# The last three slots of a fused attention and adapter kernel, put into one written order

## The chip, the cores and the metric

The kernel runs on one core of a Trainium2 chip. The metric is the device time of one execution in microseconds (us). Engines are named as the profile names them: PE (TensorE, matrix products; PEld is its weight load), DVE (VectorE), ACT (ScalarE), POOL (GpSimd) and SP (the queue engine that issues most DMAs). Each engine works through its own instructions in the order in which the program gives them and waits where an input is not there yet.

## What is computed

The reference is a spatial-reduction attention, followed by a mixture of eight low-rank adapters of which each token takes two. Cut to what matters:

```python
# attention: 4 batches of 12288 queries, 768 keys each, 128 channels
kv_flat = mean over 4x4 patches of kv, @ w_sr          # keys and values are the same
a = softmax(q @ kv_flat.T / sqrt(128))
x = a @ kv_flat                                        # (49152, 128)
# adapters
logits = x @ w_gate                                    # 8 experts, the best 2 of each token
w = softmax of the two chosen logits
out = x + sum over the 2 chosen e of w[e] * ((x @ A[e]) @ B[e])     # rank 16
```

## The kernel before

**The work is cut into 96 chunks of 512 tokens**, 24 to a batch. A chunk goes through these steps, and the names are those of the rows in the profile (all products are recorded on line 70, the helper `mm`):

- scores, in three units (`scores`, L293): two PE products of 512 columns into a PSUM tile `sg`, and one exponential on ACT (L309) from it into `em`. There are two `sg` tiles.
- attention (`attend`, L311): 24 PE products of 136 columns into `acc`, of which there is one. The columns are 128 channels, seven logits and the sum of the exponentials.
- normalise (`normalize`, L328): on DVE a reciprocal (L330) and a multiply over the whole chunk (L338) into `xn`, which holds x and the logits.
- the best two logits (`top`, L353, four DVE instructions MAX8), the routing (`route`, L362, four small POOL instructions L370 to L376 that make an argument and a mask), a tanh on ACT (L383) and two POOL instructions (L385, L386) that make the gate weights `gw`.
- x transposed: four PE products (`tx` below) into PSUM, a copy to SBUF.
- down (`down`, L431): four PE products with A, into PSUM.
- gate (`gate`, L436): DVE multiplies by the gate weights (L439), which gives `hg`.
- `hg` transposed, either by PE and a copy or by a DMA transpose issued from SP (`turn_dma`, `turn_alone`).
- up (`up`, L469): four PE products with B, into PSUM `d_ps`.
- finish (`finish`, L480): DVE adds x to the result (L486), and SP stores two chunks together (L491).

The small PSUM tiles of transposes, down and up come from a pool `mb` with two buffers. A tile that is to be written waits until a buffer has been read out.

**The order.** Chunks run as a pipeline over slots. In slot k the scores of chunk k are made, chunk k-1 is attended, chunk k-2 is normalised and its logits are routed, and the adapters of older chunks run in between. A loop (L651 to L790) emits the slots up to 95. The tail behind it (L792 to L934) takes what is left by hand. It attends chunk 95 and ends the adapters of chunks 92 to 95 in that order: routing of 95 on DVE (L907 to L912), the other gates on POOL, copies of transposes on ACT (`fetch_x` L837, `fetch_h` L843). Chunk 92's result is copied by ACT (`carry`, L866) and its x added by POOL (`add_there`, L870). DVE adds those of 93, 94 and 95 (`add_here`, L861). The four chunks are stored one by one (`store`, L476). Chunk 94's store is on ACT's queue and the other three are on SP's.

Slots 93, 94 and 95 begin at 346.3 us of the profiled execution, and the last compute instruction ends at 365.92 us.

Of the kernel before, what the change touches and what calls it, by code (L numbers as in the profile page):

```python
# [10 lines left out]
FP32 = mybir.dt.float32  # L11
BF16 = mybir.dt.bfloat16
# [8 lines left out]
def kernel(  # L21
# [87 lines left out]
    def load_q(g, m):  # L109
# [8 lines left out]
        keep(nc.sync.dma_start(q_f[g, m], src[:, m * S:(m + 1) * S]))  # L118

# [208 lines left out]
    def normalize(k):  # L328
# [3 lines left out]
        if m == 0:  # L332
            half = k0 % 2 if k0 >= TURN else 0
            if half == 0:
                used.append(k0)
            xg[k0] = ring[(len(used) - 1) % len(ring)][:, half:half + size[k0]]
# [23 lines left out]
    later = []  # L360

    def route(k0):  # L362
# [16 lines left out]
        later.append(lambda: gates(k0, n, eng, arg, mask))  # L379

# [99 lines left out]
    def finish(k):  # L480
# [5 lines left out]
        keep(nc.vector.tensor_tensor(osb[:, int(k == kb)], dp[k], xn[k][:, :, 0:C], op=ALU.add))  # L486
# [114 lines left out]
    done.append(NCHUNK - 5)  # L601
# [49 lines left out]
    for k in range(k1, NCHUNK):  # L651
# [100 lines left out]
        for x_ in kx[:1]:  # L752
# [5 lines left out]
            elif x_ in by_strip:  # L758
                gate(x_, strip(k, 0)[:, 1])
                turn_dma(k, *todo, (hgT, x_))  # L760
                todo = []
                up_at(k + 3, x_)
            elif k == NCHUNK - 1:
                turn_alone(x_)
                up(x_ - 1)
                finish(x_ - 1)
            else:
                gate(x_)
# [23 lines left out]
    K = NCHUNK - 1  # L792
    assert not units, units
    assert kh == [K - 3] and ku == [K - 4], (kh, ku)

    def flat(o):
        return o.rearrange("p a b -> p (a b)")[:, 0:T].rearrange("p (s c) -> p s c", s=S)

    def low(o):
        return (o.bitcast(BF16).rearrange("p a b -> p (a b)")[:, 0:T]  # L800
                .rearrange("p (s c) -> p s c", s=S))

    def bank(n=None):
        if n is None:
            return mtile([P, S, P], name="tail_ps")
        if n in banks:
            return banks[n]
        if n[0] == "a":
            t = ps_a.tile([P, S, 256], FP32, tag="acc", name="acc")
            for i in range(2):  # L810
                banks[f"a{i}"] = t[:, 2 * i:2 * i + 2]
        else:
            t = ps_s.tile([P, 2, T], FP32, tag="sg", name="sg")
            for i in range(2):
                banks[f"{n[0]}{i}"] = t[:, i:i + 1]
        return banks[n]

    banks = {}

    def spread(dst, lhs, rhs, lo=0, hi=S, transpose=False):  # L820
# [4 lines left out]
    def turn_x(k):  # L825
        ps = low(bank())
        xb = xn[k].bitcast(U16)[:, :, 1::2].bitcast(BF16)
        spread(ps, lambda s: xb[:, s, 0:C], id_bf, transpose=True)
        xT[k] = ps

    def turn_h(k, o, lo=0, hi=S):
        spread(low(o), lambda s: hg[k][:, s], id_bf, lo, hi, True)
        hgT[k, lo] = low(o)

    def fetch_x(k):
        sb = run.tile([P, S, P], BF16, tag="tt1", name="tt1")
        keep(nc.scalar.copy(sb, xT[k]))  # L837
        xT[k] = sb

    def fetch_h(k, lo=0, hi=S):  # L840
        if lo == 0:
            hgT[k] = run.tile([P, S, P], BF16, tag="tt1", name="tt1")
        keep(nc.scalar.copy(hgT[k][:, lo:hi], hgT[k, lo][:, lo:hi]))  # L843

    def part(k, o, js):
        for s in range(S):
            for j in js:
                mm(o[:, s, 0:VE], em[k][:, s, j], vx[k // NB][:, j, 0:VE],
                   start=(j == 0 and s % 2 == 0), stop=(j == J - 1 and s % 2 == 1))

    def down_into(k, o):
        hp[k] = flat(o)
        spread(hp[k], lambda s: xT[k][:, s], a_bf)

    def up_into(k, o, lo=0, hi=S):
        dp[k, lo] = flat(o)
        spread(dp[k, lo], lambda s: hgT[k][:, s], b_bf, lo, hi)

    def add_here(k, queue, lo=0, hi=S):
        osb = opool.tile([P, 2, S, C], FP32, tag="osb", name="osb")[:, 0, 0:hi - lo]  # L860
        keep(nc.vector.tensor_tensor(osb, dp[k, lo][:, lo:hi], xn[k][:, lo:hi, 0:C], op=ALU.add))  # L861
        store(queue, k, osb, lo, hi)

    def carry(k):
        osb = opool.tile([P, 2, S, C], FP32, tag="osb", name="osb")[:, 0]
        keep(nc.scalar.copy(osb, dp[k, 0]))  # L866
        dp[k] = osb

    def add_there(k, queue):
        keep(nc.gpsimd.tensor_tensor(dp[k], dp[k], xn[k][:, :, 0:C], op=ALU.add))  # L870
        store(queue, k, dp[k])

    def gate_part(k, lo=0, hi=S):
        if lo == 0:
            hg[k] = run.tile([P, S, P], BF16, tag="hg", name="hg")
        keep(nc.vector.tensor_tensor(  # L876
            hg[k][:, lo:hi].rearrange("p s (e r) -> p (s e) r", e=E),
            hp[k][:, lo:hi].rearrange("p s (e r) -> p (s e) r", e=E),
            gw[k][:, lo:hi].rearrange("p s e -> p (s e)")
            .unsqueeze(2).broadcast_to([P, (hi - lo) * E, RK]), op=ALU.mult))  # L880

    turn_x(K - 2)
    tanhs()
# [81 lines left out]
```

## Time and profile before

| | us |
|---|---|
| median of 3 runs | 371.83 (371.45 to 372.01) |
| span of the profiled execution, first to last instruction | 369.48 |
| slot 93 begins (first score product of chunk 93) | 346.3 |
| last DVE instruction ends | 365.92 |

The median is 2.35 us above the profiled execution's own span. That much lies around a span, and the profile does not show it. Times in rows are microseconds from the span's start, and mean durations are in ns. A row with `<-PE acc L70` in brackets or behind a bar says how long the engine was idle before and which instruction ended that wait. In tables by stretch each engine has its busy time and, in brackets, its number of instructions. An engine's instructions overlap by some 0.08 us each, so the sum of durations is larger than the busy time.

### The profile page before, as it was taken

How to read it: one execution, taken by the hardware profiler on the slowest of the kernel's cores; microseconds unless marked ns; L12 is line 12 of the kernel's file. 1: busy time of each engine (PE TensorE's matmuls, PEld its weight loads, DVE VectorE, ACT ScalarE, POOL GpSimd, SP SyncE). 2: the span in 40 equal slices, each digit the busy share in tenths (PEclk: the TensorE clock that was granted, in tenths of full speed). 3: DMA queues.
4: the chain of work that ended last, by engine and by line, in shares of the span. 5: the costliest groups of instructions: out<-in, count | busy, mean ns of one | idle time of the engine just before them, and what ended most of it. 6: DMA issues, size and time to landing. Idle time of an engine off the chain costs nothing.

```text
span 369.5 us, 11071 instructions
## 1 busy us (share of the span) xinstructions
PE 359.4 (97%) x4272; PEld 281.2 (76%) x4272; DVE 292.7 (79%) x923; ACT 292.8 (79%) x363; POOL 229.9 (62%) x519
## 2 busy tenths in 40 slices
PE   8899999999999999999999999999999999999993
PEld 4677788877878787787787787877777767777782
DVE  1347799887888888888888898888887777779795
ACT  1548986787878878888888888878879989898873
POOL 1110368889877677677768758756666766665442
PEclk9999999999999999999999999999999999999998
DMA  7989769999789999999999999999999999999723
GB/s 252 383 297 208 254 189 279 318 252 251 199 267 235 226 320 261 190 265 319 218 261 254 260 237 236 282 279 175 191 191 229 232 224 199 204 231 232 192 94 149
DMA packets 72869, 88.08 MB, mean 238 GB/s; under 512 B 51345, under 2 KB 51601, under 8 KB 72465
## 3 DMA queue, kind: packets, MB, share of 16 engines
q1 hardware_dynamic: 65728, 62.93, 68.3%
q0 software_dynamic: 6656, 24.12, 28.7%
q8 instruction: 33, 0.54, 0.6%
q10 hardware_dynamic: 432, 0.33, 0.3%
q14 instruction: 20, 0.16, 0.1%
HBM read 50.53 MB, written 36.70 MB: 236 GB/s over the span
## 4 chain that ended last, share of the span: by engine, by line
PE 88%; DMA 7%; DVE 2%; SPq 1%; issue 1%; ACT 0%; DVEq 0%; ACTq 0%
PE acc L70 35%; PE sg L70 32%; PE tt_ps L70 6%; PE d_ps L70 6%; PE h_ps L70 5%; DMA turn<-turn 4%; DMA kvr<-in_kv_dram 2%; DMA qf<-in_q_dram 2%; PE kpT_ps L70 1%; PE v_ps L70 1%; PE kfT_ps L70 1%; DVE xn L338 1%; SPq L102 1%; PE qT_ps L70 0%; DVE hg L876 0%
## 5 line engine op out<-in xcount | busy, mean ns | idle before, releaser
L309 ACT ACTIVATE em<-sg 128x1024 f16<-128x1024 f32 x288 | 283.3, 1022 | 58.0 <-PE sg L70 55.9
L70 PE MATMUL sg<-qT,kfT 128*128 128x512 bf16 x576 | 170.4, 379 | 0.4 <-ACT em L309 0.2
L70 PE MATMUL acc<-vx,em 128*128 128x136 f16 x2280 | 167.7, 223 | 0.1
L70 PEld LDWEIGHTS <-em 128*128 128x128 f16 x2304 | 146.7, 98 | 18.9 <-DVE xn L338 3.0
L338 DVE TENSOR_TENSOR xn<-acc,rinv 128x540 f32<-128x540 f32 x95 | 68.5, 721 | 3.3
L486 DVE TENSOR_TENSOR osb<-d_ps,xn 128x512 f32<-128x512 f32 x92 | 62.9, 689 | 2.7 <-PE d_ps L70 0.9
L541 POOL TENSOR_TENSOR kvr<-kvr 128x512 f32<-128x512 f32 (+1 forms) x48 | 56.9, 1200 | 0.5
L370 POOL TENSOR_TENSOR over<-xn,srt 128x64 f32<-128x64 f32 (+1 forms) x120 | 31.0, 279 | 36.0 <-DVE srt L358 34.4
L70 PEld LDWEIGHTS <-kfT 128*128 128x128 bf16 x576 | 45.2, 98 | 2.7 <-issue 0.6
L385 POOL TENSOR_TENSOR gw<-th,over 128x64 f32<-128x64 f32 (+1 forms) x60 | 17.3, 289 | 48.0 <-ACT th L383 47.5
L330 DVE RECIPROCAL rinv<-acc 128x4 f32<-128x4 f32 x95 | 17.3, 182 | 34.2 <-PE acc L70 31.4
L407 DVE COPY tts<-tt_ps 128x1024 bf16<-128x1024 bf16 (+1 forms) x73 | 36.9, 506 | 0.0
L70 PEld LDWEIGHTS <-xn 128*128 128x128 bf16 x296 | 22.5, 98 | 16.5 <-DVE xn L338 0.2
L358 DVE MAX8 srt<-xn 128x8 f32<-128x8 f32 x380 | 34.5, 153 | 0.1
L70 PEld LDWEIGHTS <-tts 128*128 128x128 bf16 x388 | 27.0, 98 | 7.0 <-DVE tts L407 0.4
L70 PE MATMUL h_ps<-a_bf,tts 128*128 128x128 bf16 x284 | 27.5, 219 | 0.0
L70 PE MATMUL tt_ps<-id_bf,xn 128*128 128x128 bf16 x284 | 27.4, 219 | 0.0
L376 POOL TENSOR_SCALAR over<-over 128x64 f32<-128x64 f32 (+1 forms) x60 | 19.8, 330 | 5.4
L229 POOL TENSOR_TENSOR kvr<-kvr 128x512 f32<-128x512 f32 x18 | 22.4, 1271 | 0.5 <-DMA kvr<-in_kv_dram 0.4
L439 DVE TENSOR_TENSOR hs<-h_ps,gw 128x512 bf16<-128x512 f32 x28 | 19.1, 683 | 4.5 <-POOL gw L386 4.0
L439 DVE TENSOR_TENSOR hg<-h_ps,gw 128x512 bf16<-128x512 f32 x26 | 17.9, 689 | 5.9 <-POOL gw L386 5.2
L70 PEld LDWEIGHTS <-turn 128*128 128x128 bf16 x176 | 13.0, 98 | 10.2 <-DMA turn<-turn 2.2
(98 smaller groups left out, 314.6 us busy)
## 6 DMA issues: line engine op xcount, KB each, us to landing
out_dram<-osb SPq DMA_DIRECT2D x46, 512.0 KB, 5.8
kvr<-in_kv_dram POOLq DMA_DIRECT2D x24, 512.0 KB, 6.6
kvr<-in_kv_dram SPq DMA_DIRECT2D x21, 512.0 KB, 7.7
qbf<-in_q_dram POOLq DMA_DIRECT2D x20, 512.0 KB, 7.7
qf<-in_q_dram SPq DMA_DIRECT2D x8, 256.0 KB, 7.4
kvr<-in_kv_dram SPq DMA_DIRECT2D x6, 256.0 KB, 7.5
qbf<-in_q_dram POOLq DMA_DIRECT2D x4, 256.0 KB, 5.6
out_dram<-osb SPq DMA_DIRECT2D x3, 256.0 KB, 2.3
```

Of the source, the lines that this page charges most:

```text
L70: return keep(nc.tensor.matmul(*a, **k))
L229: keep(adder.tensor_tensor(u[:, lo:hi], u[:, lo:hi], v[:, lo:hi], op=ALU.add))
L309: keep(nc.scalar.activation(o, i_, AF.Exp, bias=0.0, scale=scale))
L330: keep(nc.vector.reciprocal(ri, acc[k][:, :, VC]))
L338: keep(nc.vector.tensor_tensor(x[:, :, 0:VC], acc[k][:, :, 0:VC], ri.unsqueeze(2).broadcast_to([P, S, VC]), op=ALU.mult))
L358: keep(nc.vector.max(srt[k0][:, m, s], xn[k][:, s, C:C + E]))
L370: keep(eng.tensor_tensor(d, lg, so[:, :, i].unsqueeze(2).broadcast_to([P, n, 8]), op=ALU.subtract))
L376: keep(eng.tensor_scalar(mask, mask, 0.0, None, op0=ALU.is_ge))
L407: keep(nc.vector.tensor_copy(sb[:, lo:hi], ps[:, lo:hi]))
L439: keep(nc.vector.tensor_tensor(hg[k].rearrange("p s (e r) -> p (s e) r", e=E), hp[k].rearrange("p s (e r) -> p (s e) r", e=E), gw[k0][:, m ...
L486: keep(nc.vector.tensor_tensor(osb[:, int(k == kb)], dp[k], xn[k][:, :, 0:C], op=ALU.add))
L541: keep(nc.gpsimd.tensor_tensor(u, u, v, op=ALU.add))
```

## The change

The loop now ends after slot 92. All that it did in slots 93 to 95, and the whole hand-written tail, is replaced by one list of steps, `closing`, which a new function `last` works through. Each step names an operation, a chunk, and an engine or a PSUM pool. The order in which the program gives the steps is the order of each engine. What differs in content:

- The chunks are attended in the order 92, 95, 94, 93, and their scores are made in that order (95, 94, 93).
- Chunk 94 is normalised by four ACT activations (a copy with the reciprocal as scale, one for each 128 tokens), behind the reciprocal on DVE.
- Chunk 92's x reaches its result on PE. Four fp32 products with an identity matrix (`rx`) write x into the PSUM tile first, the up products accumulate onto it, and ACT copies the sum out (`fc`).
- The transposes of `hg` of chunks 90, 91 and 92 are DMA transposes (`hd`); before, this was so for 92, while 90 and 91 went over PE in one PSUM tile together with the x of 91 and 92, with one copy on DVE for both halves. The copies of the x of 91 and 92 (`cx`) are now for one half alone.
- The gate weights of 90, 92, 93 and 94 are made on DVE in one instruction, those of 91 and 95 by POOL. The routing of 92 is on DVE, and that of 95 is on POOL.
- All stores go through SP. Chunk 89 is finished before 88.

Steps: `sc` scores, `at` attention (a quarter), `nm` normalise, `top`, `rt` routing, `th` tanh, `gw` gate weights, `tx` and `cx` transpose of x and its copy, `dn` down, `gt` gate, `hd` DMA transpose of `hg`, `hx` and `ch` its transpose by PE and the copy, `up`, `ad` add x and store, `fc` copy out and store.

```diff
-    for k in range(k1, NCHUNK):
+    for k in range(k1, NCHUNK - 3):
...
-    turn_x(K - 2)
-    tanhs()
...
-    add_here(K, nc.sync)
+    def last(op, k, *w):
...
+        elif op == "nm":
...
+            keep(nc.vector.reciprocal(ri[:, lo:hi], acc[k][:, lo:hi, VC]))
+            if e is nc.scalar:
+                for s in range(lo, hi):
+                    keep(nc.scalar.activation(x[:, s, 0:VC], acc[k][:, s, 0:VC], AF.Copy, bias=0.0,
+                                              scale=ri[:, s:s + 1]))
...
+        elif op == "hd":
+            dst = hpool.tile([P, 1, S, P], BF16, tag="t1", name="t1", bufs=3)
+            keep(nc.sync.dma_start(dst.rearrange("c h s p -> c (h s) p"),
+                                   hg[k].rearrange("p s c -> p (s c)"), transpose=True))
...
+        elif op == "rx":
+            dp[k] = held("rx", k, lo, lambda: bank(pool))
+            for s in range(lo, hi):
+                mm(dp[k][:, s], id_f, xn[k][:, s, 0:C], start=(s == lo), stop=False)
...
+        elif op == "fc" and k >= NCHUNK - 4:
+            osb = out_of(k)
+            copy(e, osb[:, lo:hi], dp[k][:, lo:hi])
+            store(nc.sync, k, osb[:, lo:hi], lo, hi)
...
+    closing = (
+        "nm 91 - DVE; tx 90 - mb; sc 95 2; cx 90 - DVE; th 90 -; up 87 - mb; sc 95 0; "
+        "at 92 0 acc; at 92 1 acc; at 92 2 acc; sc 95 1; ad 87 -; at 92 3 acc; top 91 -; "
+        "rt 91 - POOL; gw 90 - DVE; tx 91 - mb; nm 92 - DVE; sc 94 2; dn 90 - mb; sc 94 1; "
+        "gt 90 -; at 95 0 acc; hd 90; at 95 1 acc; tx 92 - mb; sc 94 0; top 92 -; "
+        "cx 91 - DVE; cx 92 - DVE; th 91 -; at 95 2 acc; at 95 3 acc; gw 91 - POOL; sc 93 0; "
+        "up 89 - mb; rt 92 - DVE; dn 91 - mb; sc 93 1; nm 95 - DVE; top 95 -; th 92 -; "
+        "at 94 0 acc; at 94 1 acc; gt 91 -; ad 89 -; gw 92 - DVE; sc 93 2; dn 92 - mb; "
+        "hd 91; at 94 2 acc; at 94 3 acc; up 88 - sg; up 90 - mb; at 93 0 sg; rt 95 - POOL; "
+        "at 93 1 sg; th 95 -; gt 92 -; nm 94 - ACT; at 93 2 sg; hd 92; at 93 3 sg; ad 88 -; "
+        "tx 94 - mb; ad 90 -; tx 95 - mb; gw 95 - POOL; top 94 -; up 91 - acc; rx 92 - sg; "
+        "rt 94 - POOL; cx 95 - ACT; nm 93 - DVE; th 94 -; dn 95 - mb; top 93 -; cx 94 - ACT; "
+        "ad 91 -; tx 93 - sg; rt 93 - POOL; gw 94 - DVE; gt 95 -; up 92 - sg; cx 93 - ACT; "
+        "dn 94 - mb; th 93 -; hx 95 - acc; dn 93 - mb; fc 92 - ACT; gt 94 -; gw 93 - DVE; "
+        "ch 95 - ACT; gt 93 -; hx 94 - sg; up 95 - mb; ch 94 - ACT; hx 93 - mb; up 94 - sg; "
+        "ch 93 - ACT; ad 95 -; up 93 - acc; ad 94 -; ad 93 -")
```

More of the change, by code (lines that the diff above doesn't have):

```diff
@@ L790, with bank, spread @@
             add_patches(*w)
[L792 to L820, printed above, removed]
+    closed = {}
+    def bank(pool, dtype=FP32):
+        if pool == "mb":
+            return mtile([P, S, P], dtype, name="end_ps")
+        t = ps_a.tile([P, S, 256], FP32, tag="acc", name="end_ps") if pool == "acc" else ps_s.tile(
+            [P, 2, T], FP32, tag="sg", name="end_ps")
+        t = t.rearrange("p a b -> p (a b)")[:, 0:T]
+        if dtype is BF16:
+            t = t.bitcast(BF16)[:, 0:T]
+        return t.rearrange("p (s c) -> p s c", s=S)
+    def spread(dst, lhs, rhs, lo, hi, transpose=False):
         kw = dict(is_transpose=True) if transpose else {}
@@ L840, in fetch_h @@
[L840 to L853, printed above, removed]
```

215 lines of the change are left out of this document (122 added, 93 removed).

## The prediction

> **What bounds the kernel now.** I read the page first, then the chain that ended last, then busy time by stretches of the end, then single rows there.
>
> ```profile
> PE 359.4 (97%) x4272; PEld 281.2 (76%) x4272; DVE 292.7 (79%) x923; ACT 292.8 (79%) x363; POOL 229.9 (62%) x519
> ```
>
> Over the whole span PE is full, but the change touches only what follows 346.3 us. Three rows of busy time by stretches cover that end (length, then busy time and instructions of PE, PEld, DVE, ACT, POOL, then clock, DMA share, GB/s).
>
> ```profile
> 346.85:363.60 16.75, 15.44 (x205) 12.35 (x203) 15.07 (x50) 12.86 (x21) 7.18 (x28) 1.00 0.36 118
> 360.20:363.60 3.40, 2.26 (x28) 1.57 (x28) 3.16 (x14) 2.50 (x7) 1.66 (x6) 1.00 0.24 99
> 363.60:365.92 2.32, 1.03 (x12) 0.68 (x12) 1.99 (x4) 0.82 (x2) 0.68 (x1) 1.00 0.33 124
> ```
>
> In the first stretch DVE is busy 15.07 of 16.75 us, hardly less than PE. In the second, behind the last attention, it is busy 3.16 of 3.40, and PE only 2.26. The chain that ended last says the same (start, length, engine, tile, line):
>
> ```profile
> 359.61 0.69 DVE hg L876
> ...
> 362.91 0.70 DVE hg L876
> ...
> 363.66 0.41 PE sg L70 x4
> ...
> 364.15 0.59 ACT tt L843
> ...
> 365.23 0.69 DVE osb L861
> ```
>
> From 359.61 to 363.60 it runs on DVE: gate of 93, normalise of 95, gate of 95. From the end of the last gate there is a fixed run: transpose on PE, copy on ACT, up on PE, add on DVE, 2.32 us to 365.92. So the end is set by the time at which DVE ends its last gate, and after it by the stores.
>
> **The change, part by part.** First, DVE's list. Prices, from the groups by form (busy us, mean ns behind the bar) and from line 407 by itself (min, median and max ns; the shortest is one half, the longest a pair):
>
> ```profile
> L338 DVE TENSOR_TENSOR xn<-acc,rinv 128x540 f32<-128x540 f32 x95 | 68.5, 721 | 3.3
> ...
> L921 DVE SCALAR_TENSOR_TENSOR gw<-th,mk 128x32 f32<-128x32 f32 x1 | 0.2, 182 | 0.0
> ```
>
> ```profile
> L407 DVE COPY tts<-tt_ps x73: 414/416/693, 33.9 to 355.2; 128x512 bf16<-128x512 bf16 x49, 128x1024 bf16<-128x1024 bf16 x24
> ```
>
> Chunk 94's multiply leaves DVE: -0.72. The two copies of pairs (x of 91 with `hg` of 90, x of 92 with `hg` of 91) become copies of one half: 2 x (0.416 - 0.693) = -0.55. Gate weights come to DVE for four chunks where it had one (95): +3 x 0.18 = +0.55. Routing on DVE changes from chunk 95 to 92 and costs the same. Chunk 92's add was not on DVE before and is not after. Net -0.72 us, of which all lies ahead of the last gate.
>
> Second, the waits. I followed the new order on all engines from 346.3 us. An instruction starts when its engine is free and its inputs are there, with 0.03 to 0.15 us for a hand-over (a gate ends at 363.60, PE starts at 363.66). PE's groups take, by the chain of waits:
>
> ```profile
> 356.38 0.43 PE sg L70 x2
> 356.82 0.22 PE d_ps L70 x4
> 357.04 1.06 PE acc L70 x18
> 358.11 0.22 PE tail_ps L70 x4
> ```
>
> A score unit is 0.43, a quarter of an attention 0.35, four small products 0.22. What DVE waited for so far were the ends of attentions. Of the four reciprocals, the first (92) and the last (95):
>
> ```profile
> 350.12 0.18 DVE L330 RECIPROCAL rinv<-acc 128x4 f32<-128x4 f32 x1 [0.51 <-PE acc L70]
> ...
> 360.23 0.18 DVE L330 RECIPROCAL rinv<-sg 128x4 f32<-128x4 f32 x1
> ```
>
> In the new order `at 92` still starts when `nm 91` has freed `acc` (347.8) and has one score unit among its quarters instead of two groups. Its reciprocal comes at 349.9. `at 95` starts behind four groups of PE at 351.05 and ends its third quarter at 352.8, so that the second reciprocal comes at 353.3. `at 94` (354.4 to 356.7, two groups in between) gives 356.7. `at 93` goes to an `sg` tile, need not wait for `acc`, and ends at 358.5: the fourth reciprocal comes at 358.55, 1.7 us before the old one. It is then DVE that is late. Behind 358.55 stand the reciprocal and multiply of 93 (0.90), four MAX8 (0.37), the add of 91 (0.69), gate weights of 94, gates of 95 and 94, gate weights and gate of 93 (0.18 + 0.69 + 0.69 + 0.18 + 0.69), 4.4 us by durations, 4.1 with the overlap of neighbours. The last gate ends at 362.7. Worked in the same way, the old order's last gate ends at 363.43, where the trace has 363.60. So the difference is -0.75 us. It agrees with the budget: -0.72 of work and waits as before (1.7 us in the old list: 16.75 less 15.07). New waits of DVE that stand in it: 0.2 for `cx 92`, 0.13 for `gw 92` (its tanh stands behind an exponential on ACT; `gt 92` and all that follows are queued behind it), 0.1 for `top 95`.
>
> Third, what lies beside.
>
> `nm 94` on ACT: four activations of 128x135.
>
> ```profile
> L309 ACT ACTIVATE em<-sg 128x1024 f16<-128x1024 f32 x3 | 3.1, 1020 | 0.5 <-PE sg L70 0.5
> L837 ACT COPY tt<-tail_ps 128x512 bf16<-128x512 bf16 x2 | 1.2, 585 | 1.2 <-PE tail_ps L70 1.2
> L383 ACT ACTIVATE th<-over 128x32 f32<-128x32 f32 x2 | 0.4, 221 | 0.0
> ```
>
> On the line between the two activations, 135 elements take 221 + 103 x 0.805 = 304 ns. The upper bound is the copy, 0.585. Both ends: four take 1.0 us or 2.1 us, with 0.09 of overlap each. At 304 they end at 357.9, when DVE reaches `top 94` at 358.1 and PE reaches `tx 94` at 358.35. I take 304, the nearer rows, at no cost. Above 0.39 each, every 0.1 costs 0.44, at 0.59 it is 0.84. The Trainium skill, page "ScalarE: Activation LUTs", section "What ACT_TABLE_LOAD costs", adds about 93 ns for each pointer operand, which the scale is here. No row before the change has one. By that an activation would be an estimated 0.40, and the compute term would be -0.71 instead of -0.75.
>
> `rx 92`: four fp32 products. The nearest rows:
>
> ```profile
> 242.80 0.50 PE v_ps L70 x4
> ```
>
> ```profile
> L70 PEld LDWEIGHTS v_ps<-wext,kpT x48: 186/190/191, 11.4 to 271.3; 128*128 128x128 f32 x48
> L70 PE MATMUL v_ps<-wext,kpT x48: 278/278/319, 11.6 to 271.4; 128*128 128x135 f32 x48
> ```
>
> Each fp32 product is two records there, and two products take 0.50. So four take 0.95 at 128 columns. Upper end: with no overlap of loads, 8 x (0.28 + 0.19) = 3.8; lower end the 0.22 of bf16. I take 0.95, a measured stretch of the same kind. PE has it at 359.0 to 360.0, and `dn 95`, `tx 93`, `up 92`, `dn 94` are queued behind. DVE works off the add of 91 and gates meanwhile, and gate 93 has its input at 361.9, as DVE reaches it at 362.0. Cover is gone above 1.05, then it costs its excess, up to 2.7. Below 0.95 nothing is gained.
>
> `hd 90`, `hd 91`: two PE transposes (0.44) become DMA transposes, an issue of 1.2 on SP each.
>
> ```profile
> t<-h SPq DMA_TRANSPOSE x17, 6.8
> ```
>
> ```profile
> t<-h SPq DMA_TRANSPOSE x1, 2.4
> ```
>
> ```profile
> DMA to landing us min/median/max: 2.4/3.4/4.4
> ```
>
> The first is the median of all 17 such transposes, the second the only one behind 340 us (issued at 357.4), the third is of the last two. The new ones are issued at 351.5, 355.3 and 356.85, and are needed at 356.7, 358.8 and 360.4: slack 5.2, 3.5 and 3.5 from issue to landing. DMA share is 0.36 here. I take up to 3.4, at no cost. On SP the store of 88 and 89 now stands behind `hd 92`, at 358.1, and nobody waits for it.
>
> The order of chunks ahead, chunk 88 behind 89, and POOL's routing (7.18 of 16.75 busy) cost nothing: POOL has over half its time free, and loses the 1.27 us add of chunk 92.
>
> Fourth, the stores.
>
> ```profile
> 364.31 1.97 SPq L476 DMA_DIRECT2D out_dram<-osb  x3
> ```
>
> ```profile
> 365.00:365.50 0.50, 0.19 (x4) 0.01 (x1) 0.29 (x2) 0.00 (x0) 0.00 (x0) 1.00 0.70 270
> 365.50:366.00 0.50, 0.00 (x0) 0.00 (x0) 0.42 (x1) 0.00 (x0) 0.00 (x0) 1.00 1.00 369
> 367.50:368.00 0.50, 0.00 (x0) 0.00 (x0) 0.00 (x0) 0.00 (x0) 0.00 (x0) 0.50 0.78 303
> ```
>
> ```profile
> DMA to landing us min/median/max: 2.1/2.1/2.1
> ```
>
> ```profile
> DMA to landing us min/median/max: 2.4/2.4/2.4
> ```
>
> The last two rows are the landings of the store at 364.31 and of the last one, issued at 365.94. Four stores of 256 KB (three on SP, one on ACT's queue) leave within 1.6 us, the DMA share is 1.00 until shortly before 368, and the last lands at 368.34. By the order worked out, chunk 92's store leaves at 362, those of 95, 94 and 93 at 363.6, 364.2 and 365.0. At 370 to 390 GB/s a store takes 0.7, so that no queue is left for the last one. I take 2.1 for it, as for the first one before. That is -0.3. Ends: 0 (2.4 again), and -0.45 (the share of 0.70 puts the first bytes at 365.15, 0.84 behind the issue at 364.31; a lone store issued at 365.94 would begin at 366.8 and end at 367.5, and the share of 0.78 has the end at about 367.9). All on SP: an issue takes 0.35, and the adds come 0.69 apart, so nothing queues there.
>
> Sum: -0.75 - 0.3 = -1.05 us, a span of 368.4 against 369.48 of the profiled execution. The 2.35 us around the span stay. On the median: 371.83 - 1.05 = 370.8.
>
> **The rivals.**
>
> A, new waits eat it: the order is tight at `cx 92`, `gw 92`, `nm 94`, `rx 92` and gate 93 (0 to 0.2 us of slack each, `rx` 0.1). For: the slack is less than the error of my working (0.17). Against: it hit the old order's last gate to 0.17 over 17 us. If activations take 0.5 (+0.48) and the hand-overs on the way another 0.3, the sum is -0.3, and the time is 371.5. With nothing saved by the stores as well: 371.8. That is no change.
>
> B, slower: the DMA transposes of 91 and 92 land late. One mechanism: `up 91` and `up 92` wait on PE, and the down products of 95, 94 and 93 are queued behind them, then the gates. Every 0.1 us of landing beyond 3.5 costs 0.1. At 4.4, the upper of the last two, it is +0.85: 371.6. At 6.8, the median of all, +3.25: 374.0. From 4.6 on it is slower than before. For it: the median. Against it: in this stretch the share of DMA is a third, and the single one there took 2.4.
>
> C, more: DVE's waits shrink too, since PE is 1.7 us ahead at the fourth attention. Half of the 0.5 us of waits above gone and -0.45 from the stores: -1.45, 370.4. At most another 0.5 goes in hand-overs: 369.9.
>
> D, it doesn't do what it says: ACT's normalise or the identity product put a load of a table or separate loads in. At 3.8 us for `rx 92` it is +2.7 and 373.5. Against it are the 0.50 us row and the one table load in the whole trace:
>
> ```profile
> L178 ACT ACT_TABLE_LOAD x1 | 1.3, 1283 | 1.6 <-PEq L949 1.6
> ```
>
> **How the numbers follow.** 0.2% is 0.74 us, about what a measurement of this kernel can tell from no change: below 371.09 is faster, above 372.57 slower. Forecast (370.3 to 371.1): 0.48. C (369.9 to 370.3): 0.12. A (371.1 to 372.2): 0.26. B 0.09 and D 0.05, of which 0.03 together land within 0.2%: they give 0.11 of slower. So faster 0.60, same 0.29, slower 0.11. The likeliest is the forecast, 370.8. The range goes from 369.9 to 372.2: it leaves out B and D beyond that and little more, and it takes in both ends of `nm 94` and of the stores, and the first 1.3 us of `rx 92`'s excess and of late transposes.
>
> **What would show it.** In the changed kernel: the fourth reciprocal near 358.6 and DVE without gaps above 0.2 from there to the last gate, near 362.7 to 362.9; the last add ending near 365.2; four activations of near 0.31 to 0.40 between 357 and 358.5; `rx 92` within 1.0; the transposes issued near 355.3 and 356.9 landing before 358.8 and 360.4; a last store that lands 2.1 after its issue. I am wrong if PE waits for a transpose, if DVE waits more than 0.5 in one place behind 356, or if the last store takes 2.4 or more again.

## The result, and the profile after

The changed kernel takes 371.1 us (median of 22 runs) beside 372.21 for the kernel before in the same session (22 runs). The ratio is 0.9963, with a 95% interval from 0.9945 to 0.9982: faster by 0.37%, where the forecast was 0.28% (1.05 of 371.83). In a second session the same kernel gave 0.9933 [0.9901, 0.9964]. Ratios are of the fast runs alone, and three profiled executions below (the changed kernel again, 93 and 95 swapped, and the kernel before without a store) are slow ones, but the granted clock is 1.00 in every closing that is compared here. The profiled execution has a span of 368.51, where 368.4 was forecast and 369.48 stood before. So size and sign came out as forecast. The terms of the sum did not, and the experiments are about them.

First the page and busy time by stretches of the changed kernel, cut at the same events as in the prediction (length, then busy time and instructions of PE, PEld, DVE, ACT, POOL, clock, DMA share, GB/s):

```profile
PE 360.2 (98%) x4272; PEld 282.2 (77%) x4272; DVE 291.8 (79%) x925; ACT 293.6 (80%) x367; POOL 226.9 (62%) x511
```

```profile
346.94:363.22 16.28, 15.66 (x202) 12.61 (x200) 14.21 (x51) 13.65 (x25) 4.95 (x20) 1.00 0.51 138
...
363.22:365.48 2.26, 1.07 (x14) 0.67 (x12) 1.98 (x3) 0.77 (x2) 0.00 (x0) 1.00 0.55 210
```

From the reciprocal of chunk 91 to the last gate it is 16.28 us instead of 16.75. DVE's work in it fell from 15.07 to 14.21, by 0.86. (The budget had -0.72. By durations it is 0.77, and the rest is that neighbours overlap more.) But DVE now stands idle for 2.07 instead of 1.68. Only about half of the saved work turned into time. The rows of the timeline show where DVE and PE waited (start, length, engine, line, tile, and in brackets the idle time before it and what ended it):

```profile
346.94 0.17 DVE L847 RECIPROCAL rinv<-acc 128x4 f32<-128x4 f32 x1
...
349.99 0.18 DVE L847 RECIPROCAL rinv<-acc 128x4 f32<-128x4 f32 x1 [0.82 <-PE acc L70]
353.42 0.18 DVE L847 RECIPROCAL rinv<-acc 128x4 f32<-128x4 f32 x1 [0.32 <-PE acc L70]
356.89 0.17 DVE L847 RECIPROCAL rinv<-acc 128x4 f32<-128x4 f32 x1
357.09 1.16 ACT L850 ACTIVATE xn<-acc,rinv 128x135 f32<-128x135 f32 x4
358.67 0.18 DVE L847 RECIPROCAL rinv<-sg 128x4 f32<-128x4 f32 x1
359.36 0.40 PE L70 MATMUL end_ps<-b_bf,t 128*128 128x128 bf16 x4 [0.28 <-DMA t<-h]
359.59 1.11 PE L70 MATMUL end_ps<-xn,id_f 128*128 128x128 f32 x8
360.54 0.39 PE L70 MATMUL end_ps<-a_bf,tts 128*128 128x128 bf16 x4
...
360.96 1.36 DVE L902 TENSOR_TENSOR hg<-end_ps,gw 128x512 bf16<-128x512 f32 x2 [0.26 <-PE end_ps L70]
362.53 0.69 DVE L902 TENSOR_TENSOR hg<-end_ps,gw 128x512 bf16<-128x512 f32 x1
363.35 2.13 DVE L935 TENSOR_TENSOR osb<-end_ps,xn 128x512 f32<-128x512 f32 x3
```

The four reciprocals come at 349.99, 353.42, 356.89 and 358.67, each within 0.2 of the forecast. Then PE stands still for 0.28 in front of `up 91`, and the bracket names the cause: the DMA transpose of chunk 91's `hg`. The down products of 95, which are behind it on PE, are late, and DVE waits 0.26 for them. The last gate ends at 363.22, outside the forecast 362.7 to 362.9. The transpose that PE waited for, and the last store (issue to landing):

```profile
DMA to landing us min/median/max: 3.9/3.9/3.9
```

```profile
DMA to landing us min/median/max: 2.0/2.0/2.0
```

The store left at 365.51 and landed in 2.0, where the last one before took 2.4. The bytes end soon after 367, as busy time by half microseconds shows:

```profile
364.50:365.00 0.50, 0.25 (x4) 0.07 (x2) 0.35 (x2) 0.00 (x0) 0.00 (x0) 1.00 0.19 74
365.00:365.50 0.50, 0.00 (x0) 0.00 (x0) 0.48 (x1) 0.00 (x0) 0.00 (x0) 1.00 0.97 365
...
366.50:367.00 0.50, 0.00 (x0) 0.00 (x0) 0.00 (x0) 0.00 (x0) 0.00 (x0) 0.50 0.97 381
367.00:367.50 0.50, 0.00 (x0) 0.00 (x0) 0.00 (x0) 0.00 (x0) 0.00 (x0) 0.50 0.13 45
```

Three stores share that stretch now, not four. From the end of the last add to the span's end it is 3.03 us (365.48 to 368.51), where it was 3.56 (365.92 to 369.48).

**How the experiments are read.** The two ratios above, for one and the same program, lie 0.3% apart, nearly as much as the whole change. So ratios can't order the variants below. Profiled executions also differ by up to 8 us in when slots 93 to 95 begin, for kernels with the same instructions ahead of them. So I count from the start of the reciprocal of chunk 91 on DVE, which opens the closing part ("the closing" from here on) in both kernels. Of the kernel before:

```profile
346.85 0.17 DVE L330 RECIPROCAL rinv<-acc 128x4 f32<-128x4 f32 x1
```

By this measure, the kernel before and the same kernel without one store (below) agree within 0.01 us up to the last add, though one closing begins 7.5 us later than the other. The table has what each closing gave, in us after that reciprocal (end of the last gate, end of the last add, end of the span), PE's wait for chunk 91's transpose, and the landing of that transpose. The last column has the start and the duration of a DMA packet that is explained under "Why the transpose is late".

| kernel | last gate | last add | span end | span end less last add | PE waits | landing of 91 | packet |
|---|---|---|---|---|---|---|---|
| before | 16.75 | 19.07 | 22.63 | 3.56 | | | |
| changed | 16.28 | 18.54 | 21.57 | 3.03 | 0.28 | 3.9 | 9.5, 1.25 |
| changed, again | 15.94 | 18.19 | 21.24 | 3.05 | 0 | 3.6 | 9.5, 0.93 |
| normalise 94 on DVE | 16.37 | 18.63 | 21.66 | 3.03 | 0 | 3.7 | 9.6, 0.94 |
| add of 92 on DVE | 16.49 | 18.75 | 21.79 | 3.04 | 0.44 | 4.1 | 9.6, 1.32 |
| store of 92 late | 16.43 | 18.69 | 22.26 | 3.57 | 0.44 | 4.1 | 9.4, 1.42 |
| up of 91 late | 16.12 | 18.38 | 21.41 | 3.03 | 0 | 3.7 | 9.5, 0.93 |
| 93 and 95 swapped | 16.46 | 18.73 | 21.77 | 3.04 | 0.47 | 4.1 | 9.6, 1.41 |
| before, no store of 92 | 16.75 | 19.07 | 22.29 | 3.22 | | | |
| long warm-up | 15.85 | 18.11 | 21.16 | 3.05 | 0 | 2.4 | 6.9, 1.20 |
| long warm-up, add of 92 on DVE | 16.45 | 18.71 | 21.75 | 3.04 | 0 | 2.4 | 6.9, 1.27 |
| long warm-up, gate weights on POOL | 16.60 | 18.86 | 21.91 | 3.05 | 0 | 2.4 | 7.0, 1.22 |
| short products in the warm-up | 15.84 | 18.11 | 21.16 | 3.05 | 0 | 2.4 | 6.9, 0.99 |
| no warm-up | 16.27 | 18.54 | 21.59 | 3.05 | 0.29 | 3.9 | 10.4, 0.97 |

PE comes to `up 91` at 12.1 in the changed kernel, and the transpose is issued at 8.4. So the landing may take 3.7 before PE waits.

### The profile page after: what moved, and what is told of

It reads as the page before. It is cut to its first block, busy times and chain, and to the rows that moved or that the text cites. A ratio compares the mean times of both kernels' runs of the same rounds, so it can differ in the third digit from the quotient of the medians.

```text
span 368.5 us, 11062 instructions
## 1 busy us (share of the span) xinstructions
PE 360.2 (98%) x4272; PEld 282.2 (77%) x4272; DVE 291.8 (79%) x925; ACT 293.6 (80%) x367; POOL 226.9 (62%) x511
## 4 chain that ended last, share of the span: by engine, by line
PE 88%; DMA 8%; DVE 1%; SPq 1%; ACT 0%; issue 0%; DVEq 0%
PE acc L70 35%; PE sg L70 32%; PE tt_ps L70 6%; PE d_ps L70 5%; PE h_ps L70 5%; DMA turn<-turn 4%; DMA kvr<-in_kv_dram 2%; DMA qf<-in_q_dram 2%; PE kpT_ps L70 1%; PE v_ps L70 1%; PE end_ps L70 1%; DMA out_dram<-osb 1%; PE kfT_ps L70 1%; SPq L102 1%; PE qT_ps L70 0%
## 5 line engine op out<-in xcount | busy, mean ns | idle before, releaser
L341 DVE TENSOR_TENSOR xn<-acc,rinv 128x540 f32<-128x540 f32 x91 | 65.6, 720 | 3.1
L493 DVE TENSOR_TENSOR osb<-d_ps,xn 128x512 f32<-128x512 f32 x87 | 59.5, 689 | 2.7 <-PE d_ps L70 0.7
L373 POOL TENSOR_TENSOR over<-xn,srt 128x64 f32<-128x64 f32 (+1 forms) x112 | 29.2, 281 | 34.5 <-DVE srt L361 32.9
L389 POOL TENSOR_TENSOR gw<-th,over 128x64 f32<-128x64 f32 (+1 forms) x55 | 16.0, 292 | 43.0 <-ACT th L387 42.7
L411 DVE COPY tts<-tt_ps 128x1024 bf16<-128x1024 bf16 (+1 forms) x70 | 35.1, 501 | 0.0
L361 DVE MAX8 srt<-xn 128x8 f32<-128x8 f32 x364 | 33.0, 153 | 0.0
L70 PE MATMUL h_ps<-a_bf,tts 128*128 128x128 bf16 x272 | 26.3, 219 | 0.0
L70 PE MATMUL tt_ps<-id_bf,xn 128*128 128x128 bf16 x272 | 26.3, 219 | 0.0
L379 POOL TENSOR_SCALAR over<-over 128x64 f32<-128x64 f32 (+1 forms) x56 | 18.7, 333 | 5.0
L443 DVE TENSOR_TENSOR hg<-h_ps,gw 128x512 bf16<-128x512 f32 x24 | 16.5, 689 | 5.8 <-POOL gw L390 5.2
```

What stands on the lines that cost most here:

```text
L70: return keep(nc.tensor.matmul(*a, **k))
L341: keep(nc.vector.tensor_tensor(x[:, :, 0:VC], acc[k][:, :, 0:VC], ri.unsqueeze(2).broadcast_to([P, S, VC]), op=ALU.mult))
L361: keep(nc.vector.max(srt[k0][:, m, s], xn[k][:, s, C:C + E]))
L373: keep(eng.tensor_tensor(d, lg, so[:, :, i].unsqueeze(2).broadcast_to([P, n, 8]), op=ALU.subtract))
L379: keep(eng.tensor_scalar(mask, mask, 0.0, None, op0=ALU.is_ge))
L411: keep(nc.vector.tensor_copy(sb[:, lo:hi], ps[:, lo:hi]))
```

## The experiments

**Theory 1** is that of the prediction: DVE's list of work sets the last gate, so each 0.1 put on DVE costs about 0.1. **Theory 2**, the rival, is that the order of PE's groups set it (an earlier fourth attention), and that what moved off DVE was worth nothing. Beside them stand two questions: whether the stores gave what the last part of the gain needs, and why chunk 91's transpose was late.

**The changed kernel again**, unaltered.

> The changed kernel once more, unaltered, as the measure for its neighbours: span 368.5 (profiled so far), last gate at 363.2, last add ending at 365.5, last store landing 2.0 after its issue. If the DMA transpose of chunk 91 lands in 3.0 instead of 3.9 us (351.6, 355.4 and 357.0 are the issues), PE does not wait for it at 359.4, and the last gate comes 0.3 earlier: then span 368.2.

Ratio 0.9933 [0.9901, 0.9964]. This time no row has PE waiting for a transpose, and the last gate and the adds are 0.34 earlier:

```profile
351.90 0.17 DVE L847 RECIPROCAL rinv<-acc 128x4 f32<-128x4 f32 x1
```

```profile
367.15 0.69 DVE L902 TENSOR_TENSOR hg<-end_ps,gw 128x512 bf16<-128x512 f32 x1
367.97 2.12 DVE L935 TENSOR_TENSOR osb<-end_ps,xn 128x512 f32<-128x512 f32 x3
```

The last gate ends at 367.84, which is 15.94 after 351.90. The landing was 3.6 here and 3.9 in the first profile. The expectation had 3.0 for a landing without a wait, and 3.6 turned out to be early enough. One program, two closings 0.34 apart: the wait comes and goes with the landing, and where it is absent the compute term is -0.81 (16.75 to 15.94), a little more than the -0.75 of the forecast.

**Normalise 94 on DVE.**

```diff
-  ... th 95 -; gt 92 -; nm 94 - ACT; at 93 2 sg; hd 92; ...
+  ... th 95 -; gt 92 -; nm 94 - DVE; at 93 2 sg; hd 92; ...
```

> Chunk 94 is normalised on DVE again, one multiply of 0.72, instead of four activations on ACT; nothing else changes. Theory 1 (DVE's list sets the last gate): the last gate comes 0.4 to 0.6 later than in the changed kernel (0.72 of work, less some of DVE's waits), the span is 368.9 to 369.1. Theory 2 (the gain is the order of PE's work, DVE has room): the gate stays within 0.1, the span within 0.1 of 368.5.

Ratio 0.998 [0.9947, 1.0014]; the interval is too wide to tell. The closing tells:

```profile
347.79 0.17 DVE L847 RECIPROCAL rinv<-acc 128x4 f32<-128x4 f32 x1
```

```profile
363.47 0.69 DVE L902 TENSOR_TENSOR hg<-end_ps,gw 128x512 bf16<-128x512 f32 x1
```

The last gate ends at 364.16, 16.37 after. Beside the closings that also had no wait (15.94, 15.85, 15.84) that is 0.43 to 0.53 more, of 0.72 put on DVE. Theory 1 holds, with part of the work taken up by closer overlap on DVE (its busy time grew by 0.48 over the second run of the changed kernel, 14.13 to 14.61). Theory 2 has no place for it. No run has DVE's old list in the new order of PE, so what the order alone is worth is not measured.

**The add of 92 on DVE**, without the identity product and ACT's copy.

```diff
-  ... up 91 - acc; rx 92 - sg; rt 94 - POOL; ... dn 93 - mb; fc 92 - ACT; gt 94 -; ...
+  ... up 91 - acc; rt 94 - POOL; ... dn 93 - mb; ad 92 -; gt 94 -; ...
```

> Chunk 92's x is added by DVE (0.69) in the place of ACT's copy; the four identity products (0.95 on PE) are gone. Theory 1: last gate 0.4 to 0.6 later, span 368.9 to 369.1, although PE has 0.95 less to do. Theory 2 (PE sets the end): PE gets to the down products of 94 and 93 earlier, so the last gate comes up to 0.3 earlier, span 368.2.

Ratio 0.9942 [0.9912, 0.9971]. The last gate is at 16.49. PE waited 0.44 for the transpose:

```profile
359.14 0.40 PE L70 MATMUL end_ps<-b_bf,t 128*128 128x128 bf16 x4 [0.44 <-DMA t<-h]
```

Two other kernels with a wait of 0.44 and 0.47, which left `rx 92` in place, ended at 16.43 and 16.46. So beside its like this one cost 0.03 to 0.06, and alone it looked like a point for theory 2. But it changed two things: 0.69 on DVE, and 0.95 off PE right behind the wait. A PE that is late through the wait gets that time back. The pair had to be tried without the wait, which is done below.

**93 and 95 swapped** in every step of the list.

> Chunks 93 and 95 change names in the whole list: 93 is attended second and 95 last, all else is alike (same engines, same places). Theory 1 (only what each engine does, and when, counts): span within 0.1 of 368.5, same gates. If the chunk attended first matters as such (its scores, its place in memory or in a pair): another time, either way.

Ratio 0.9973 [0.9949, 0.9996], the last gate at 16.46 with a wait of 0.47. The store-late kernel, whose compute part is that of the changed kernel in its written order, ended at 16.43 with a wait of 0.44. Which chunk is attended last is worth nothing. The place in the order is what counts.

**The store of 92 late**, behind the add of 94.

```diff
-  ... dn 93 - mb; fc 92 - ACT; gt 94 -; ... ad 95 -; up 93 - acc; ad 94 -; ad 93 -
+  ... dn 93 - mb; gt 94 -; ... ad 95 -; up 93 - acc; ad 94 -; fc 92 - ACT; ad 93 -
```

> ACT's copy of chunk 92's result, and so its store, moves from before the copies of the last three transposes to behind them: four stores of 256 KB leave within 2 us again instead of three. Theory 1 with the stores' term: last gate and last add unchanged within 0.1, the last store lands 2.4 to 2.5 after its issue instead of 2.0, span +0.4 (368.9). If the term is not real: landing stays 2.0, span within 0.1.

Ratio 0.9991 [0.9954, 1.0028]. From the last add to the span's end it is 3.57, against 3.03 in the changed kernel and 3.56 before. The share of the DMA engines, by half microseconds, and the landing of the last store:

```profile
366.50:367.00 0.50, 0.04 (x1) 0.00 (x0) 0.42 (x1) 0.07 (x1) 0.00 (x0) 1.00 0.85 332
...
368.50:369.00 0.50, 0.00 (x0) 0.00 (x0) 0.00 (x0) 0.00 (x0) 0.00 (x0) 0.50 0.97 381
369.00:369.50 0.50, 0.00 (x0) 0.00 (x0) 0.00 (x0) 0.00 (x0) 0.00 (x0) 0.50 0.70 279
```

```profile
DMA to landing us min/median/max: 2.5/2.5/2.5
```

The bytes of four stores now run until after 369.3, over 2 us past the last add (367.26). One chunk's store moved behind the add of 94, and the whole second term of the sum went back. So the number of stores in the last stretch counts. In the eleven other closings of the new order, with three stores there, this part is 3.03 to 3.05.

**Before, without the store of 92** (its output is not written).

```diff
-        store(queue, k, dp[k])
```

> The kernel before, without the store of chunk 92 (that part of the output is not written); its copy and add stay. Three stores instead of four stand in the last 1.6 us. If the queue of stores costs what the changed kernel saved there: last add still at 365.9, the last store lands 1.9 to 2.1 after its issue instead of 2.4, span 369.0 to 369.2 against 369.48. If not: landing 2.4, span 369.4 to 369.5.

Ratio 1.0017 [0.9978, 1.0057]. Up to the last add nothing changed (19.07 in both). From there it is 3.22 instead of 3.56: -0.34. The last store lands in 2.0, as expected, so one store fewer gives all of the landing's 0.4, and about two thirds of the changed kernel's 0.53. The other 0.19 lies behind the last landing: the span ends 1.17 after it here and 1.11 in the kernel before, where all closings of the new order have 0.99 or 1.00. No run shows the cause of that. Chunk 94's store is on ACT's queue in the two kernels of the old order alone, which no run changes by itself.

**Up of 91 late**: behind `rx 92` and the down products of 95, and the add of 91 behind `gt 95`.

```diff
-  ... top 94 -; up 91 - acc; rx 92 - sg; ... th 94 -; dn 95 - mb; ... cx 94 - ACT; ad 91 -; ... gt 95 -; ...
+  ... top 94 -; rx 92 - sg; ... th 94 -; dn 95 - mb; up 91 - acc; ... cx 94 - ACT; ... gt 95 -; ad 91 -; ...
```

> The up products of chunk 91, which waited on PE for a DMA transpose (landing 3.9 against 3.5 of slack), go behind the identity products and the down products of 95; the add of 91 goes behind the gate of 95. If that wait was what kept the last gate at 363.2: PE has no wait for the transpose, the gate comes 0.1 to 0.3 earlier, span 368.2 to 368.4. If DVE's list sets it in any case: gate and span within 0.1.

Ratio 0.998 [0.9947, 1.0012]. No wait, with a landing of 3.7, and the last gate at 16.12. That is 0.16 before the changed kernel with its 0.28 of wait, and 0.18 behind it without. So this order costs 0.18 where there is no wait. Whether it takes a wait away this run can't show: at a landing of 3.7 the kernel with 94 normalised on DVE, which has `up 91` in its old place, does not wait either. The interval can't show a difference of this size.

**Why the transpose is late.** I looked for what lies beside it. On the page's part on DMA queues (packets, MB, share of 16 engines' span) one queue of the changed kernel has few and large packets, 16 KB each:

```profile
q8 instruction: 33, 0.54, 0.6%
```

The same table for the 5.5 us from 8.0 after the reciprocal of 91, in the changed kernel, with DMA's busy tenths and GB/s above it (40 slices of 0.14 us):

```profile
DMA  0000000000066999990000000000699982009999
GB/s 0 0 0 0 0 0 0 0 0 0 0 138 145 199 207 199 110 11 0 0 7 7 11 9 9 11 8 9 121 177 223 212 172 40 0 0 417 417 417 387
...
q8 instruction: 1, 0.02, 1.4%
```

Chunk 91's bytes come at 200 GB/s and break off. Then 6 to 11 GB/s trickle for over 1 us, then those of 92 come at 200 again. One packet of the instruction queue takes 1.4% of 16 engines for 5.5 us, that is about 1.2 us of one engine. It starts at 356.5, as the bytes of 91 begin. 0.54 MB over PE's 8544 instructions (4272 products and as many weight loads) is 63 bytes each, so one packet would be the fetch of about 260 of PE's instructions. If so, another number of PE instructions ahead moves it. At the 402 instructions in 16.28 us of this stretch, 64 more make it come 2.6 us earlier.

**Long warm-up.** The 8 products that warm PE up at the start become 40 of 102 columns each, which makes 64 more instructions.

```diff
-        for _ in range(n):
-            mm(mtile([P, T], name="spin_ps"), zero[:, 0:P], zero, start=True, stop=True)
+        m = 5 if n == 8 else 1
+        for _ in range(m * n):
+            mm(mtile([P, T], name="spin_ps")[:, 0:T // m], zero[:, 0:P], zero[:, 0:T // m], ...)
```

> The changed kernel with PE's first eight spin products of 512 columns written as forty of 102: as many columns, 64 PE instructions more at the very start, nothing else. In the runs so far the DMA transpose of chunk 91 landed 3.6 to 4.1 us after its issue, that of 90 in 2.4; with 91's a 16 KB packet of the instruction queue was under way, and the later the landing, the longer that packet. Theory 3 (that packet, a fetch of PE's program on one of the 16 DMA engines, holds up one sixteenth of the transpose): 64 instructions move the fetches by about 2.7 us, 91's transpose lands in 2.4 to 2.8, PE does not wait for it, and from the first reciprocal (chunk 91) the last gate ends after 15.9 us and the span after 21.2, against 16.3 and 21.6 in the first profile. Rival (the transpose is late because of what SP does or because another transpose follows 1.6 us later): 3.6 to 4.1 again.

Ratio 1.007 [1.0042, 1.0099]. In the same 5.5 us of its closing the table has no row of the instruction queue, and the trickle between the bytes of 91 and those of 92 is gone. The busy tenths there, and the landings of the three transposes:

```profile
DMA  0000000000008999500000029999300569999998
```

```profile
DMA to landing us min/median/max: 2.4/2.4/2.4
```

All three transposes of the closing land in 2.4, PE doesn't wait, and the last gate comes at 15.85:

```profile
351.27 0.17 DVE L848 RECIPROCAL rinv<-acc 128x4 f32<-128x4 f32 x1
...
366.43 0.69 DVE L903 TENSOR_TENSOR hg<-end_ps,gw 128x512 bf16<-128x512 f32 x1
```

The packet starts at 6.9 now, 2.6 earlier as worked out, and the steps around the transpose stand where they stood (it is issued at 8.43, against 8.44). So the cause of the late landing is the packet. But the kernel is slower. The warm-up took 6.06 us instead of 3.59, and the packet ahead has come earlier as well: chunk 90's reciprocal to that of 91 is 4.58 here and 3.70 in the changed kernel. A later kernel's trace (short products) shows why.

**Long warm-up with the add of 92 on DVE**, and **with the gate weights of 90, 92 and 94 on POOL** (`gw 90 - POOL; gw 92 - POOL; gw 94 - POOL`), one run each, so there is no ratio.

> On top of the 64 instructions: chunk 92's x is added by DVE again, no identity products. With PE waiting for the DMA transpose this cost nothing that could be seen (last gate 16.49 against 16.46 and 16.43 us after the first reciprocal in runs with the same wait). Theory 1: without that wait DVE sets the gate, and it ends 0.4 to 0.6 later than in the kernel with the 64 instructions alone (16.4 to 16.5 against 15.9). Theory 2: no difference, or earlier.

> On top of the 64 instructions: the gate weights of 90, 92 and 94 are made by POOL again (two instructions of 0.25 each) instead of one of 0.18 on DVE. If DVE's work alone counted, the last gate would come up to 0.55 earlier (15.4 us after the first reciprocal). If the hand-overs count (tanh on ACT to POOL 0.15, two instructions 0.58, POOL to DVE 0.05, against 0.25 on DVE), gates 92 and 94 wait 0.5 to 0.6 each: last gate 1.1 to 1.2 later (17.0 to 17.1).

The add, without a wait, has its last gate at 16.45: +0.60 for 0.69 put on DVE.

```profile
353.52 0.17 DVE L848 RECIPROCAL rinv<-acc 128x4 f32<-128x4 f32 x1
...
369.28 0.69 DVE L903 TENSOR_TENSOR hg<-end_ps,gw 128x512 bf16<-128x512 f32 x1
```

That settles the earlier miss. Theory 1 holds here as well, and theory 2 falls. The gate weights on POOL have it at 16.60: +0.75, though three instructions of 0.18 were taken off DVE. Two gates on DVE now wait for POOL:

```profile
360.97 0.69 DVE L903 TENSOR_TENSOR h<-end_ps,gw 128x512 bf16<-128x512 f32 x1 [0.71 <-POOL gw L888]
...
366.27 0.69 DVE L903 TENSOR_TENSOR hg<-end_ps,gw 128x512 bf16<-128x512 f32 x1 [0.58 <-POOL gw L888]
```

Busy time from the reciprocal of 91 to the last gate, with the gate weights on DVE and then on POOL:

```profile
351.27:367.12 15.85, 15.49 (x202) 12.60 (x200) 14.04 (x51) 13.69 (x25) 4.97 (x20) 1.00 0.46 142
```

```profile
351.25:367.85 16.60, 15.52 (x202) 12.61 (x200) 13.68 (x49) 13.77 (x25) 6.37 (x26) 1.00 0.48 150
```

DVE's work fell by 0.36 only, since the small instructions overlap their neighbours, and its idle time grew by 1.11 (1.81 to 2.92). The difference is the 0.75. The direction is as expected and the size smaller. The three gate weights on DVE, which the sum had as +0.55 of work, are a gain of 0.75.

**Short products in the warm-up**: 4 of 512 columns and 36 of 32 by 32.

```diff
+        big = 4 if n == 8 else n
-        for _ in range(n):
+        for _ in range(big):
             mm(mtile([P, T], name="spin_ps"), zero[:, 0:P], zero, start=True, stop=True)
+        for _ in range(9 * (n - big)):
+            mm(mtile([P, T], name="spin_ps")[0:32, 0:32], zero[:, 0:32], zero[:, 0:32], ...)
```

> The changed kernel with the warm-up at the start made of 4 products of 512 columns and 36 small ones of 32 by 32, in place of 8 of 512: again 64 more PE instructions ahead of the end, so that the fetches of PE's program fall elsewhere, but this time with little or no longer start (the 40 of 102 columns took 6.06 us for 3.59). If the late landing of chunk 91's transpose comes from a fetch that shares a DMA engine with it, the transpose lands in 2.4 us, PE does not wait, and the closing, from the reciprocal of chunk 91, has its last gate at 15.85 to 15.95 and its span end at 21.1 to 21.2, as with the longer warm-up; the warm-up takes 2.5 to 4.5 us by an estimate of 0.05 to 0.10 for a small product, and the time is 370.0 to 371.0 (ratio 0.994 to 0.997), a gain over the changed kernel that its interval can hardly show. If instead the longer start itself had made the difference, the landing is 3.6 to 4.1 again, and the last gate comes at 15.94 to 16.5.

Ratio 1.0041 [0.9992, 1.009]. The warm-up did not get shorter: 6.21 us, about 0.12 for a small product. So the start is as long as with the long warm-up, and this run does not separate the packet from a longer start by itself. The closing is again the one without a wait (15.84, landing 2.4). What separates the two is in the rows ahead of the closing: the reciprocal of chunk 90 (that of 91 is at 349.20), the last two transposes issued ahead of that of 91 on SP's queue (issue to landing), and PE's waits for the second of them (us in total, times, longest):

```profile
344.60 0.18 DVE L336 RECIPROCAL rinv<-acc 128x4 f32<-128x4 f32 x1 [0.75 <-PE acc L70]
```

```profile
DMA to landing us min/median/max: 3.1/4.0/5.0
```

```profile
PEld L70 <- DMA turn<-turn: 0.9, 1, 0.9
...
PE h_ps L70 <- DMA turn<-turn: 0.7, 1, 0.7
```

In the changed kernel the same two transposes land in 3.3 and 3.4, and PE doesn't wait for them. One packet of the instruction queue lies in the flight of the transpose that took 5.0, and none in that of the closing, which took 2.4. In the changed kernel it is the other way round, 3.3 and 3.9. So the late landing goes with the packet, and not with the start. From the reciprocal of 90 to the last gate it is 4.60 + 15.84 = 20.44 here, 3.70 + 16.28 = 19.98 in the changed kernel, 3.70 + 15.94 = 19.64 in its second run and 3.71 + 16.75 = 20.46 before. Moving the fetch gave 0.4 behind the reciprocal of 91 and took 0.9 ahead of it. It is no way to a faster kernel, and a closing by itself would have hidden that.

**No warm-up**: the 8 products left out, 16 instructions fewer.

```diff
-        "spin 8; proj1; spin 3; proj2; ...
+        "proj1; spin 3; proj2; ...
```

> The changed kernel without the 8 warm-up products at its very start (their result is used nowhere; the 3 further on stay). PE has 16 instructions fewer ahead of the end, so by the pace at the end (256 instructions, one fetch of 16 KB, in about 11 us) the fetches come some 0.7 us later against the work: at 10.2 after the reciprocal of chunk 91 instead of 9.5, when most of the bytes of chunk 91's transpose have passed, and the fetch before it at -0.2, where no transpose is under way. In the two kernels with the longer warm-up the fetch had moved 2.6 the other way, and there fell upon the transpose ahead of the closing (landing 5.0, and 4.58 from the reciprocal of 90 to that of 91 instead of 3.70). If the place of the fetch is the cause, both are spared here: 3.70 between those reciprocals, 91's transpose lands in 2.6 to 3.3, PE does not wait for it, and the last gate comes at 15.85 to 15.95 after the reciprocal of 91, 0.3 to 0.4 earlier than in the changed kernel. If the fetch is not the cause, the landing stays at 3.6 to 4.1. What the start does without the warm-up no run shows: between 3.6 us less and some us more by a slower clock; the time is 369.5 to 372 if it is within a microsecond of the old one.

Ratio 0.9976 [0.9952, 1.0001]. The packet starts at 10.4 after the reciprocal of 91, 0.8 later than in the changed kernel, and the interval ahead is 3.71: both as expected. The landing of 91's transpose is not. PE waits 0.29, and the last gate is at 16.27:

```profile
DMA to landing us min/median/max: 3.9/3.9/3.9
```

A shift of 0.8 us is not enough to clear the transpose, which is under way from 8.4 to 10.8 when nothing disturbs it. In the eight closings where the packet falls into that time, the landing is 3.6 to 4.1, and in the four where it doesn't, 2.4. Among the seven with a start of 9.4 to 9.6, a packet of 0.93 or 0.94 goes with a landing of 3.6 to 3.7, and one of 1.3 to 1.4 with 4.1. What its start adds is not settled: a packet of 0.97 that starts at 10.4 made the landing 1.5 later here, and one of 0.93 at 9.5 made it 1.2 later. At the start, leaving the warm-up out costs 0.9 (one early reciprocal is at 30.57 instead of 29.66). So no version here beats the changed kernel by more than an interval.

## Why the prediction was right, and where it was not

**The bound: right.** DVE's list sets the last gate. 0.72 put back costs 0.43 to 0.53, and 0.69 costs 0.60, where PE has no wait: 0.06 to 0.09 for each 0.1. The reciprocals came within 0.2 of the times worked out.

**The compute term, -0.75: half right.** Undisturbed it is -0.81 to -0.91 (15.94 to 15.84 against 16.75), of a budget that gave -0.72 and a trace that has -0.86 of DVE's work. With the late transpose it is -0.47, and 0.34 to 0.44 are lost. (The prediction's own two times, 362.7 and 363.43, differ by 0.73.) DVE's waits stayed near the old 1.68, as assumed: 1.81 where PE does not wait.

**The step that failed is `hd 91`: "I take up to 3.4, at no cost".** Its landing was 3.6 to 4.1 in each of the seven profiles of the new order that left the start as it was, and PE waited for it in four of them, 0.28 in the first. The slack was 3.7 in the trace and not 3.5, and what the landing took beyond that, up to 0.4, PE waited. Rival B's mechanism came true, at the lower end of its range (a landing of 3.9 cost 0.34, where B's rule gives 0.4) and not as the whole result. The prediction had "the share of DMA is a third" as the argument against it. The share was 0.51 in the changed kernel, and 0.46 with the long warm-up, where the same transpose landed in 2.4. So a mean share says nothing about a single packet that holds one engine for a microsecond. The test named for being wrong ("if PE waits for a transpose") fired, and the total came to the forecast since the stores gave more than their term.

**The stores, -0.30 with ends 0 and -0.45: right in kind, mis-sized.** It is -0.53 from the last add to the span's end (3.56 to 3.03), past the end of the range, of which 0.4 is the landing (2.4 to 2.0) and the rest lies behind it. The store of 92 alone is -0.34 (left out of the old order) and +0.54 (put back late).

**`nm 94` on ACT: between the two prices.** The row of the four activations by itself:

```profile
L850 ACT ACTIVATE xn<-acc,rinv x4: 366/372/382, 357.1 to 357.9; 128x135 f32<-128x135 f32 x4
```

0.372 each, where the interpolation gave 0.304. The Trainium skill, page "ScalarE: Activation LUTs", section "What ACT_TABLE_LOAD costs", led to 0.40 by its term for a pointer operand, and it came nearer. It cost nothing either way: they end at 358.25, and DVE, which uses them next, was busy with two adds until then (357.03 to 358.32).

**`rx 92`: right.** PE has it from 359.59 to the next group at 360.54, 0.95.

**Gate weights on DVE: mis-priced by themselves.** The budget counted +0.55 of work and no wait for POOL in the new order. In that order they save 1.11 of waits for 0.36 of work, 0.75 net. The term is still near, since the budget compared with the old order, whose gates stood elsewhere.

**The sum.** Compute -0.53 (19.07 to 18.54 at the last add, the wait in it) and stores -0.53 make -1.06, against -0.75 - 0.30 = -1.05. Two errors of 0.22 and 0.23 went opposite ways, and that they cancel so closely is luck. The second run, without the wait, has -0.88 and -0.51, which make -1.39. Of the rivals, D is out (one table load as before, `rx 92` in 0.95). C came about in its part on the stores, and not in DVE's waits. A's price for slower activations was not paid.

## What to carry to other kernels

When two kernels differ by less than their runs vary, measure from an event that both have, near the place of the change, and then check the stretch ahead of that event too: what a closing gains can be paid just before it. Slack against a DMA transpose should be set by the slowest landing that the trace has nearby (4.4 here), not by the mean load of the DMA engines. When an experiment moves two resources at once, as the add did (DVE up, PE down), repeat it with the other wait gone before a theory is dropped.

## What the runs showed of the hardware

- PE's program seems to be fetched in packets of 16 KB that share the DMA engines with the kernel's own transfers: 33 in the span, 0.9 to 1.4 us each amid transposes, one in about 11 us at the end. 64 instructions more moved one from 9.5 to 6.9 after the reciprocal of 91, and 16 fewer to 10.4. That it is PE's program is inferred from these moves and from 63 bytes an instruction. No run shows its content. A transpose in flight beside one landed in 3.6 to 5.0 us instead of 2.4 and 3.3.
- 36 products of 32 by 32 took about 0.12 us each at the start (6.21 less four of 0.45), hardly less than 40 of 102 columns at 0.15 (6.06). Fewer columns do not make a product there much shorter.
- Without the warm-up the first products of the kernel are slower. The same group of 32 took 6.07 us, where it took 4.06 with it, though the granted clock is 1.00 in the rows of both. In the changed kernel a product of this group takes 0.27 from 7.3 us on, and without the warm-up 0.42 until 10.8 us (changed kernel first):

```profile
6.49 4.06 PE L70 MATMUL kpT_ps<-id_f,kvr 128*128 128x128 f32 x32
```

```profile
6.10 6.07 PE L70 MATMUL kpT_ps<-id_f,kvr 128*128 128x128 f32 x32
```
